# A new order of instructions for lightning attention followed by a gated MLP: step 2's keys and queries ahead of step 1's values

## The chip, the core and the metric

One core of a Trainium2 chip runs the program. Its engines have queues of their own and work side by side: TensorE (PE, with its weight loads shown as PEld), VectorE (DVE), ScalarE (ACT), GpSimd (POOL) and SyncE (SP), which here only issues DMAs. PSUM is TensorE's output memory, in eight banks; SBUF is the working memory. The metric is the device time of one execution in microseconds, from the first to the last instruction and a little around it.

## What is computed

The reference, cut to what matters. Inputs are q, k, v of 4 batches, 8 heads, 768 tokens and 64 columns, in float32:

```python
for b in range(nb):                                   # blocks of 64 tokens
    intra = np.einsum('bhic,bhjc->bhij', qb, kb) * Dmask[None]
    intra = np.einsum('bhij,bhjd->bhid', intra, vb)
    inter = np.einsum('bhid,bhde->bhie', qb * lam_pow[None], kv_state)
    out[:, :, sl] = intra + inter
    kv_state = lam_block[None, :, None, None] * kv_state + np.einsum('bhsd,bhse->bhde', kb_dec, vb)
...
x = np.ascontiguousarray(attn_out.transpose(0, 2, 1, 3)).reshape(B, S, H * D)
h = np.maximum(x @ w_in, 0.0)                         # 512 -> 1024
u, v = (h[..., :d_ff // 2].copy(), h[..., d_ff // 2:].copy())
v_n = (v - mu) / np.sqrt(var + 1e-06)                 # over the 512 columns
v_s = np.einsum('ts,bsd->btd', w_spatial, v_n) + b_spatial[None, :, None]
gated = u * v_s
return (gated @ w_out).astype(np.float32)
```

So attention with a decaying state comes first, then a layer whose normalized half is mixed over all 768 tokens of a batch by W_spatial.

## The kernel before

The tokens are cut into 12 steps of 256, three for each of the four batches; step n belongs to batch n // 3. Everything is written by small functions, one for each kind of work, and the string ORDER at the top of the file calls them one after the other: `KM.2.1.D` is the function k_m for step 2, part 1, on VectorE. The last letter names the engine (T TensorE, D VectorE, A ScalarE, P GpSimd, S SyncE), the last numbers of work on PSUM are banks. Each engine runs its own work strictly in the order of this string, and waits where data or a buffer isn't there yet. So ORDER alone decides what stands behind what.

The names, in the order in which a step uses them:

- LK, LQ, LV: loads of k, q and v of a step, 512 KB each, all on the SP queue (line 195). There are three buffers for each, so step 3 reuses those of step 0. WH: four loads of 512 KB of W_in; 0 and 1 are the half for v, 3 and 2 that for u. WQ: six loads of W_spatial, WP: W_out.
- KM, QM (line 330): scale half of a step's keys or queries by the decay and cast them to bf16 (kc, qc). VC: cast of v (vb); VD: the same in two halves. CW, CX, WC: casts of W_in and W_spatial.
- TK, TQ (line 365): transposes on TensorE into PSUM, and EK, EQ: copies of these to SBUF (kT, qT). From step 6 on DK and DQ do the transposes by DMA instead.
- SC (line 395): scores; MK (line 400): their mask, on VectorE; KP (line 424): the state's increments; SX, SY, SA: the states. AV (lines 458 and 467): the attention's output; EX: its copy to SBUF (xT). FN reads one element of a bank and holds its engine until AV's part is done.
- PV (line 492): x @ W_in for the half v; EV: its relu (vh); BN, RA, RD, RB: mean, variance, 1 / sqrt(var + eps), and -mean times that; VN: the normalized half (vn), on VectorE (line 531) or ScalarE (line 528), two to a step. PU (line 543) and EU: the half u (uT).
- WT and EW: transposes of W_spatial, once. GP: bias into a bank; PW (line 569): the spatial product over the batch's six vn tiles, eight for each batch; GM (line 575): times u (gT). PO and PH (lines 580 and 589), EO and EH, ST and SH: the output product, its copy and its store.
- FL (line 308): matmuls of ones whose result nobody reads.

A PV matmul reads both halves that EX writes: PV.n.0 first that of EX.n.0, PV.n.1 first that of EX.n.1. The vn of a batch are all needed by each of its PW; the matmuls of one PW read them in the order of the tokens.

Of the kernel before, what the change touches and what calls it, by code (L numbers as in the profile page):

```python
# [13 lines left out]


ORDER = """
lam.A BR.A tab.0.A LQ.0.S LK.0.S LQ.1.S LV.0.S LK.1.S LV.1.S LK.2.S LQ.2.S WH.0.S WH.1.S posk.P msk.P idn.P eps.D
one.D row.D FL.1.512.3.1.T FL.1.512.0.1.T LB.0.T FL.1.512.1.1.T FL.1.512.1.1.T FL.1.512.2.1.T FL.1.256.5.1.T
BB.1.6.T BB.0.1.T LN.0.A LL.D LX.A KM.0.1.D QM.0.0.P TQ.0.0.4.T QM.0.1.D KM.0.0.D TQ.0.1.3.T TK.0.0.2.T TK.0.1.5.T
FL.1.512.0.1.T EQ.0.0.4.D mkc.D EQ.0.1.3.D EK.0.1.5.D QM.1.1.D QM.1.0.P BE.0.1.A BE.1.6.A EK.0.0.2.A tab.1.A  # L20
SC.0.0.1.2.T MK.0.0.1.2.D VC.0.P KP.0.4.T SC.0.1.5.6.T TQ.1.0.0.T KM.1.0.P KM.1.1.P TQ.1.1.2.T TK.1.0.1.T
FL.1.512.3.1.T FL.1.512.3.1.T FL.1.256.3.1.T SX.0.A SY.0.4.A SA.0.1.D MK.0.1.5.6.D KM.2.1.D TK.1.1.3.T
FL.1.512.4.1.T EQ.1.0.0.A AV.0.0.5.6.T EQ.1.1.2.A EK.1.0.1.A FN.0.5.6.A EK.1.1.3.A VD.1.1.P VD.1.0.P KP.1.4.T
SC.1.0.0.1.T SY.1.4.D AV.0.1.5.6.T FL.1.512.2.1.T FL.1.512.2.1.T KM.2.0.P SC.1.1.3.4.T FL.1.512.2.1.T MK.1.0.0.1.D
QM.2.0.P QM.2.1.P CW.2.P EX.0.1.6.A EX.0.0.5.A TK.2.1.6.T FL.1.512.0.1.T FL.1.256.1.1.T TK.2.0.2.T TQ.2.0.5.T
FL.1.256.0.1.T TQ.2.1.1.T SA.1.1.D MK.1.1.3.4.D EQ.2.0.5.D CW.0.D SA.1.0.D EK.2.1.6.A EK.2.0.2.A AV.1.0.6.3.T
SC.2.0.4.5.T MK.2.0.4.5.D EQ.2.1.1.A LV.2.S WH.3.S WH.2.S LK.3.S FN.1.6.3.A CW.1.A SC.2.1.0.1.T AV.1.1.6.3.T CW.3.A
PV.0.0.2.T PV.0.1.4.T CX.1.P MK.2.1.0.1.D EV.0.1.4.D EX.1.0.6.A EX.1.1.3.A PV.1.0.5.T PV.1.1.0.T VC.2.A GP.0.3.0.3.A
KP.2.6.T AV.2.0.1.4.T EV.0.0.2.D BN.0.0.D EV.1.0.5.A FN.2.1.4.A EV.1.1.0.A SA.2.0.D BN.0.1.D RA.0.A GP.0.0.0.6.D
BN.1.1.D BN.1.0.D RD.0.D RB.0.D PU.1.1.2.T AV.2.1.1.4.T PU.0.1.5.T EX.2.1.4.A EX.2.0.1.A PV.2.1.0.T EU.1.1.2.A  # L30
RA.1.A EV.2.1.0.A LQ.3.S CX.0.P PU.1.0.4.T EU.1.0.4.A EU.0.1.5.A PV.2.0.1.T EV.2.0.1.A QM.3.1.D BN.2.1.D VN.0.1.D
BN.2.0.D WQ.1.S WQ.0.S WQ.2.S WC.2.D KM.3.0.P KM.3.1.P PU.0.0.2.T WC.0.A EU.0.0.2.A QM.3.0.P TK.3.2.0.T TQ.3.2.4.T
EQ.3.2.4.A PU.2.1.5.T WC.1.P WT.2.0.1.T WT.0.0.2.T WT.1.0.4.T EK.3.2.0.D RD.1.D RA.2.A EW.2.0.1.D RD.2.D VN.1.1.D
VN.1.0.D VN.0.0.D VN.2.1.D VN.2.0.D EW.0.0.2.A EW.1.0.4.A PU.2.0.0.T WQ.5.S LV.3.S WQ.3.S WQ.4.S EU.2.0.0.D VC.3.A
GP.0.2.0.0.A EU.2.1.5.A GP.0.1.0.5.A SC.3.1.1.2.T PW.0.0.0.6.T PW.0.3.0.3.T WC.5.P MK.3.1.1.2.D WC.3.D WC.4.P LK.4.S
LQ.4.S WP.S LV.4.S LQ.5.S PW.0.2.0.0.T WT.0.1.4.T WT.1.1.1.T WT.2.1.2.T PW.0.1.0.5.T QM.4.0.P QM.4.1.P WX.1.P
GM.0.3.0.3.D KM.4.0.D EW.1.1.1.D GM.0.0.0.6.D EW.0.1.4.A GP.0.2.1.3.A EW.2.1.2.A PW.0.2.1.3.T KP.3.4.T SC.3.0.1.2.T
GM.0.2.0.0.D GP.0.1.1.6.D GM.0.1.0.5.D SX.3.A GP.0.3.1.0.A SY.3.4.A WX.0.A GP.0.0.1.5.D KM.4.1.D MK.3.0.1.2.D
PW.0.1.1.6.T PW.0.0.1.5.T GM.0.1.1.6.D GM.0.0.1.5.D TQ.4.2.4.T PW.0.3.1.0.T GM.0.2.1.3.D SA.3.1.D GM.0.3.1.0.D
EQ.4.2.4.A TK.4.2.1.T EK.4.2.1.A PO.0.0.5.T EO.0.0.5.A VC.4.P QM.5.0.P LK.5.S KM.5.0.P KM.5.1.P QM.5.1.D PO.0.2.4.T  # L40
EO.0.2.4.D AV.3.0.6.2.T KP.4.3.T SC.4.0.0.1.T SY.4.3.D FN.3.6.2.A AV.3.1.6.2.T SC.4.1.4.5.T EX.3.0.6.A EX.3.1.2.A
PO.0.3.3.T SA.4.0.D MK.4.0.0.1.D TQ.5.2.6.T PV.3.1.2.T TK.5.2.0.T LV.5.S PV.3.0.1.T EO.0.3.3.A EQ.5.2.6.A LQ.6.S
LV.6.S LK.6.S LK.7.S LQ.7.S EV.3.1.2.A SA.4.1.D MK.4.1.4.5.D EK.5.2.0.D VC.5.P KM.6.1.P KM.6.0.P LV.7.S LK.9.S
LQ.8.S LK.8.S AV.4.0.4.0.T SC.5.0.2.3.T FN.4.4.0.A EV.3.0.1.A SC.5.1.5.6.T KP.5.6.T KM.7.0.P QM.6.1.P QM.7.0.P
QM.7.1.P KM.7.1.P GN.2.1.P QM.6.0.D MK.5.1.5.6.D AV.4.1.4.0.T PO.0.5.1.T PU.3.1.5.T EX.4.1.0.A EX.4.0.4.A PV.4.0.6.T
PV.4.1.0.T BN.3.0.D MK.5.0.2.3.D VC.6.A EO.0.5.1.D SA.5.0.D AV.5.0.4.2.T FN.5.4.2.A EV.4.0.6.A KP.6.3.T AV.5.1.4.2.T
PU.4.1.1.T PO.0.1.6.T EX.5.0.4.A EU.3.1.5.D EX.5.1.2.A PV.5.0.4.T BN.3.1.D EV.4.1.0.D BN.4.0.D SY.6.3.D BN.4.1.D
EU.4.1.1.D EV.5.0.4.A PV.5.1.5.T PO.0.4.2.T EO.0.1.6.A EV.5.1.5.A RA.4.A PU.4.0.0.T PU.5.0.3.T PU.3.0.4.T PU.5.1.1.T
BN.5.0.D GP.1.1.0.6.D BN.5.1.D EO.0.4.2.A RD.4.D VN.4.0.D GP.1.0.0.5.A GP.1.2.0.2.A RA.3.A RD.3.D RB.3.D RA.5.A
# [36 lines left out]

# [556 lines left out]
```

## Time and profile before

| | us |
|---|---|
| median of 3 runs | 142.25 (141.66 to 143.23) |
| profiled execution | 142.2 |
| its span, first to last instruction | 140.5 |
| TensorE busy in the span | 132.7 (94%) |
| VectorE busy | 114.8 (82%) |
| ScalarE busy | 80.1 (57%) |
| GpSimd busy | 55.1 (39%) |

The profile names a line of the file, an engine, an operation and its tiles. Busy time of TensorE contains its fillers (FL). In the chain of waits each piece is either an engine's work or a transfer; it shows what the end hung on, step by step back from the last instruction. The DMA share of a stage is the mean over 16 DMA engines.

### The profile page before, as it was taken

How to read it: one execution, taken by the hardware profiler on the slowest of the kernel's cores; microseconds unless marked ns; L12 is line 12 of the kernel's file. 1: busy time of each engine (PE TensorE's matmuls, PEld its weight loads, DVE VectorE, ACT ScalarE, POOL GpSimd, SP SyncE). 2: the span in 40 equal slices, each digit the busy share in tenths (PEclk: the TensorE clock that was granted, in tenths of full speed). 3: DMA queues.
4: the chain of work that ended last, by engine and by line, in shares of the span. 5: the costliest groups of instructions: out<-in, count | busy, mean ns of one | idle time of the engine just before them, and what ended most of it. 6: DMA issues, size and time to landing. Idle time of an engine off the chain costs nothing.

```text
span 140.5 us, 4680 instructions
## 1 busy us (share of the span) xinstructions
PE 132.7 (94%) x1967; PEld 84.6 (60%) x1983; DVE 114.8 (82%) x229; ACT 80.1 (57%) x160; POOL 55.1 (39%) x64
## 2 busy tenths in 40 slices
PE   5999979998999999999999999999999999999990
PEld 2367654787566657648666466586555645866540
DVE  2199889999999899999488799779899799986660
ACT  4167677799567577359532278697114476962011
POOL 5268655942578177700861419605800000000000
PEclk9999999999999999999999999999999999999999
DMA  3999999999999999998903699999865980000174
GB/s 88 345 347 347 384 370 356 379 369 357 368 346 329 325 306 277 301 161 200 285 4 76 166 347 354 283 241 218 325 175 79 364 306 7 5 2 0 41 295 186
DMA packets 56729, 34.12 MB, mean 243 GB/s; under 512 B 13827, under 2 KB 51971, under 8 KB 56708
## 3 DMA queue, kind: packets, MB, share of 16 engines
q1 hardware_dynamic: 56560, 33.69, 81.4%
q8 instruction: 15, 0.25, 0.7%
q10 hardware_dynamic: 148, 0.13, 0.3%
q14 instruction: 6, 0.05, 0.2%
HBM read 24.38 MB, written 6.29 MB: 218 GB/s over the span
## 4 chain that ended last, share of the span: by engine, by line
PE 82%; SPq 6%; DMA 5%; DVE 2%; POOL 1%; issue 1%; ACT 1%; ACTq 0%; POOLq 0%
PE ps L569 23%; PE ps L492 15%; PE ps L543 15%; PE ps L580 14%; SPq L195 6%; DMA q_in<-in_q_dram 5%; PE ps L467 4%; PE ps L395 3%; PE ps L458 3%; PE ps L365 2%; PE ps L424 2%; POOL qc L330 1%; DVE vn L531 1%; PE ps L555 1%; PE ps L589 1%
## 5 line engine op out<-in xcount | busy, mean ns | idle before, releaser
L569 PE MATMUL ps<-wt_sb,vn 128*128 128x384 bf16 x192 | 33.0, 326 | 0.4 <-DVE vn L531 0.4
L400 DVE TENSOR_TENSOR a_sb<-ps,m 128x1024 bf16<-128x1024 f32 x24 | 28.7, 1216 | 1.0 <-PE ps L395 0.8
L569 PEld LDWEIGHTS <-vn 128*128 128x128 bf16 x192 | 18.3, 98 | 12.2 <-DVE vn L531 0.7
L330 POOL TENSOR_TENSOR qc<-q_in,lqn 128x512 bf16<-128x512 f32 x18 | 19.5, 1099 | 14.0 <-DMA q_in<-in_q_dram 7.7
L543 PE MATMUL ps<-xT,win_sb 128*128 128x256 bf16 x192 | 23.1, 273 | 0.0
L492 PE MATMUL ps<-win_sb,xT 128*128 128x512 bf16 x92 | 22.5, 379 | 0.3 <-issue 0.2
L580 PE MATMUL ps<-wout_sb,gT 128*128 128x512 bf16 x82 | 21.3, 380 | 0.6 <-issue 0.2
L575 DVE TENSOR_TENSOR gT<-ps,uT 128x384 bf16<-128x384 f32 x32 | 16.7, 551 | 5.7 <-PE ps L569 5.6
L543 PEld LDWEIGHTS <-win_sb 128*128 128x128 bf16 x192 | 18.4, 98 | 3.9
L330 POOL TENSOR_TENSOR kc<-k_in,lv 128x512 bf16<-128x512 f32 x18 | 18.9, 1064 | 2.8 <-DMA k_in<-in_k_dram 1.4
L180 ACT ACTIVATE o_sb<-ps 128x512 f32<-128x512 f32 (+1 forms) x16 | 9.2, 580 | 17.4 <-PE ps L580 9.9
L507 DVE BATCH_NORM_STATS2 st<-vh 128x6 f32<-128x512 bf16 x24 | 16.4, 683 | 1.0 <-ACT vh L497 0.8
L180 ACT ACTIVATE ps<-bsp 128x384 f32<-128x384 f32 x23 | 11.1, 489 | 8.5 <-DVE gT L575 7.7
L180 ACT ACTIVATE xT<-ps 128x512 bf16<-128x512 f32 x23 | 12.5, 592 | 5.3 <-PE ps L467 5.3
L492 PEld LDWEIGHTS <-xT 128*128 128x128 bf16 x96 | 9.0, 98 | 9.5 <-ACT xT L180 1.3
L580 PEld LDWEIGHTS <-gT 128*128 128x128 bf16 x92 | 8.5, 98 | 9.1
L184 POOL CAST vb<-v_in 128x1024 bf16<-128x1024 f32 (+1 forms) x9 | 8.6, 964 | 12.8 <-PE ps L467 7.8
L497 ACT ACTIVATE vh<-ps 128x512 bf16<-128x512 f32 x18 | 10.5, 593 | 3.2 <-PE ps L492 3.2
L467 PE MATMUL ps<-a_sb,vb 64*64 64x128 bf16 x384 | 9.9, 217 | 0.0
L395 PE MATMUL ps<-qT,kT 64*64 64x128 bf16 x384 | 9.8, 226 | 0.0
L497 ACT ACTIVATE uT<-ps 128x512 bf16<-128x512 f32 x16 | 9.2, 589 | 0.3 <-PE ps L543 0.3
L395 PEld LDWEIGHTS <-kT 64*64 64x64 bf16 x384 | 6.9, 111 | 1.9 <-issue 1.3
(77 smaller groups left out, 168.8 us busy)
## 6 DMA issues: line engine op xcount, KB each, us to landing
q_in<-in_q_dram SPq DMA_DIRECT2D x12, 512.0 KB, 7.0
k_in<-in_k_dram SPq DMA_DIRECT2D x12, 512.0 KB, 6.4
v_in<-in_v_dram SPq DMA_DIRECT2D x12, 512.0 KB, 6.3
out_dram<-o_sb SPq DMA_DIRECT2D x23, 256.0 KB, 3.0
wst<-in_moe_w_in_dram SPq DMA_DIRECT2D x4, 512.0 KB, 8.2
wst<-in_moe_w_spatial_dram SPq DMA_DIRECT2D x4, 384.0 KB, 6.5
wst<-in_moe_w_out_dram SPq DMA_DIRECT2D x1, 1024.0 KB
wss<-in_moe_w_spatial_dram SPq DMA_DIRECT2D x2, 384.0 KB, 6.1
```

The lines of the kernel that those rows point to most:

```text
L180: nc.scalar.activation(out=o, in_=i, func=AF.Copy)
L330: vec(e).tensor_tensor(out=dst[n % NCA][:, u].rearrange("p u m o d -> p o (u m) d"), in0=src[n % NIN].rearrange("p (o u) m d -> p o u m d" ...
L395: nc.tensor.matmul(out=pa[o][row(c), w, j], lhsT=kT[n % NTR][row(o), u, j, c * Q64:(c + 1) * Q64], rhs=qv(n, o, u, c), start=(w == 0 and j ...
L400: nc.vector.tensor_tensor(out=a_sb[n % NA][:, i].rearrange("p o w j x -> p o w (j x)"), in0=ps[:, b0:b1 + 1:b1 - b0].rearrange("p o (w y) ...
L467: nc.tensor.matmul(out=po[c ^ o][row(w), c, i], lhsT=vb[n % NCA][row(c), 4 * o + u, j, :], rhs=a[row(c), i, o, w, j, :], start=(r == 0 and ...
L492: nc.tensor.matmul(out=bank(b), lhsT=x[:, slot(c, g)], rhs=win_sb[:, g, DH:DFF], start=(g == 0), stop=(g == NCH - 1))
L497: nc.scalar.activation(out=o, in_=i, func=AF.Relu)
L507: nc.vector.bn_stats(out=st6[p2][:, t], in_=vh[p2][:, t])
L543: nc.tensor.matmul(out=pu[:, f2].rearrange("p (c x) -> p c x", c=2), lhsT=win_sb[:, g, f * P:(f + 1) * P], rhs=x[:, slot(0, g):slot(1, g) ...
L569: nc.tensor.matmul(out=bank(b)[:, 0:HW], lhsT=vn[bb % 2][:, s, f * P:(f + 1) * P], rhs=wt_sb[:, s, i * HW:(i + 1) * HW], start=False, stop ...
L575: nc.vector.tensor_tensor(out=gT[bb % 2][:, f, cols], in0=bank(b)[:, 0:HW], in1=uT[bb % 2][:, f, cols], op=ALU.mult)
L580: nc.tensor.matmul(out=bank(b), lhsT=gT[bb % 2][:, f, t * P:(t + 1) * P], rhs=wout_sb[:, f, :], start=(f == 0), stop=(f == NCH - 1))
```

## The change

Only ORDER changes: the functions are the same (one empty line less at the top moves all line numbers down by one). All engines get a new order. Counted over the string:

| kind | before | after |
|---|---|---|
| VN | 18 on VectorE, 6 on ScalarE | 14 and 10 |
| EV | 6 on VectorE, 18 on ScalarE | 11 and 13 |
| EX | 1 on VectorE, 23 on ScalarE | 3 and 21 |
| EO | 8 on VectorE, 15 on ScalarE | 10 and 13 |
| EU | 8 on VectorE, 16 on ScalarE | 9 and 15 |
| EQ | 3 on VectorE, 6 on ScalarE | 5 and 4 |
| QM | 6 on VectorE, 18 on GpSimd | 3 and 21 |
| WC | 2 VectorE, 1 ScalarE, 3 GpSimd | 0, 2 and 4 |
| VD | 2 GpSimd | 1 GpSimd, 1 ScalarE |
| CX | 2 GpSimd | 1 GpSimd, 1 ScalarE |
| FL | 17 on TensorE | 10 |

Two lines of the table, the ones with the first loads:

```diff
-lam.A BR.A tab.0.A LQ.0.S LK.0.S LQ.1.S LV.0.S LK.1.S LV.1.S LK.2.S LQ.2.S WH.0.S WH.1.S posk.P msk.P idn.P eps.D
+lam.A BR.A tab.0.A msk.P idn.P posk.P LK.0.S LQ.0.S LQ.1.S LV.0.S eps.D one.D row.D FL.1.512.1.1.T FL.1.256.0.1.T
```

The SP queue from its start, before; q_in, k_in and v_in with their buffer's number are the loads of the steps, wst_0 and wst_1 take W_in:

```order
L195 DMA q_in_0_90<-in_q_dram 128x8x128
L195 DMA k_in_0_93<-in_k_dram 128x8x128
L195 DMA q_in_1_91<-in_q_dram 128x8x128
L195 DMA v_in_0_96<-in_v_dram 128x8x128
L195 DMA k_in_1_94<-in_k_dram 128x8x128
L195 DMA v_in_1_97<-in_v_dram 128x8x128
L195 DMA k_in_2_95<-in_k_dram 128x8x128
L195 DMA q_in_2_92<-in_q_dram 128x8x128
L252 DMA wst_0_141<-in_moe_w_in_dram 128x2x512 x2
L195 DMA v_in_2_98<-in_v_dram 128x8x128
L252 DMA wst_1_142<-in_moe_w_in_dram 128x4x256 x2
L195 DMA k_in_0_93<-in_k_dram 128x8x128
```

The same stretch after:

```order
L194 DMA k_in_0_93<-in_k_dram 128x8x128
L194 DMA q_in_0_90<-in_q_dram 128x8x128
L194 DMA q_in_1_91<-in_q_dram 128x8x128
L194 DMA v_in_0_96<-in_v_dram 128x8x128
L194 DMA k_in_1_94<-in_k_dram 128x8x128
L194 DMA k_in_2_95<-in_k_dram 128x8x128
L194 DMA q_in_2_92<-in_q_dram 128x8x128
L194 DMA v_in_1_97<-in_v_dram 128x8x128
L251 DMA wst_0_141<-in_moe_w_in_dram 128x2x512 x2
L251 DMA wst_1_142<-in_moe_w_in_dram 128x4x256
L194 DMA v_in_2_98<-in_v_dram 128x8x128
L194 DMA q_in_0_90<-in_q_dram 128x8x128
```

v_in_1 (LV.1) goes from the sixth to the eighth place, k_in_2 and q_in_2 move up one each, and the first of the two loads into wst_1 moves ahead of v_in_2.

ScalarE ahead of the first PV, before; qT, kT are EQ and EK, seen2 is FN, xT is EX, win_sb is CW:

```order
L180 ACTIVATE seen2_73<-ps_61 1x1
L180 ACTIVATE kT_1_106<-ps_61 128x512
L180 ACTIVATE xT_0_115<-ps_61 128x4x128 x2
L180 ACTIVATE kT_0_105<-ps_61 128x512 x2
L180 ACTIVATE qT_0_107<-ps_61 128x512
L180 ACTIVATE seen2_73<-ps_61 1x1
L180 ACTIVATE win_sb_84<-wst_0_141 128x512 x2
L180 ACTIVATE xT_1_116<-ps_61 128x4x128 x2
```

The same place after:

```order
L179 ACTIVATE seen2_73<-ps_61 1x1
L179 ACTIVATE vb_1_104<-v_in_1_97 128x512
L179 ACTIVATE xT_0_115<-ps_61 128x4x128 x2
L179 ACTIVATE kT_0_105<-ps_61 128x512 x2
L179 ACTIVATE seen2_73<-ps_61 1x1
L179 ACTIVATE win_sb_84<-wst_0_141 128x512 x2
L179 ACTIVATE xT_1_116<-ps_61 128x4x128 x2
```

Half of the cast of v_in_1 (VD.1.0) came to ScalarE, ahead of both EX of step 0, both EK of step 2 and two CW; the copy qT_0 (EQ.2.1) left for VectorE.

ScalarE ahead of batch 2's first PW, before; vh is EV, uT is EU, rstd is RA, vn is VN, o_sb is EO, ps<-bsp is GP, ysb is SY:

```order
L497 ACTIVATE vh_0_118<-ps_61 128x512
L180 ACTIVATE ysb_0_139<-ps_61 128x256
L180 ACTIVATE o_sb_8_134<-ps_61 128x512
L497 ACTIVATE vh_0_118<-ps_61 128x512
L528 ACTIVATE vn_0_120<-vh_0_118,nmr_0_75,rstd_0_81 128x512 x2
L512 ACTIVATE rstd_0_81<-mv_0_79,eps_t_74 128x2
L497 ACTIVATE uT_0_122<-ps_61 128x2x256
L528 ACTIVATE vn_0_120<-vh_0_118,nmr_0_75,rstd_0_81 128x512
L180 ACTIVATE ps_61<-bsp_88 128x384
```

The same place after:

```order
L496 ACTIVATE vh_0_118<-ps_61 128x512
L496 ACTIVATE uT_0_122<-ps_61 128x2x256
L511 ACTIVATE rstd_0_81<-mv_0_79,eps_t_74 128x2
L496 ACTIVATE vh_0_118<-ps_61 128x512
L179 ACTIVATE ps_61<-bsp_88 128x384
L527 ACTIVATE vn_0_120<-vh_0_118,nmr_0_75,rstd_0_81 128x512 x2
L511 ACTIVATE rstd_0_81<-mv_0_79,eps_t_74 128x2
L179 ACTIVATE o_sb_8_134<-ps_61 128x512
L527 ACTIVATE vn_0_120<-vh_0_118,nmr_0_75,rstd_0_81 128x512
L179 ACTIVATE ps_61<-bsp_88 128x384
```

Between EV.8.0 (the first row) and ScalarE's last v_n of the batch, now VN.8.0 and before VN.8.1, stand one EU, two RA, one EV, one GP, one EO and two other v_n; before, between EV.8.0 and VN.8.1, one SY, one EO, one EV, two other v_n, one RA and one EU. On VectorE RB.8, which VN on ScalarE needs, stands behind VN.6.0, RD.8 and VN.6.1. On TensorE, between the batch's last PV (PV.8.1) and its first PW, stand PU.8.0, PO.1.2, PU.7.0, PU.6.0 and PU.8.1; before there were five PU.

131 lines of the change are left out of this document (65 added, 66 removed).

## The prediction

> **What bounds the kernel now.** I read the page's first two parts, then busy time by stage, then the chain of work that ended last, then the order of time up to the first dense matmuls, and last the place where TensorE meets VectorE and ScalarE before a spatial product. Busy time by stage, with the columns stretch, its length, PE, PEld, DVE, ACT and POOL busy, clock, DMA share, GB/s:
>
> ```profile
> 14.00:18.78 4.78, 4.02 (x128) 2.66 (x126) 4.24 (x7) 2.92 (x6) 3.67 (x4) 1.00 1.09 375
> 18.78:20.77 1.99, 1.83 (x84) 1.56 (x86) 1.45 (x3) 1.56 (x4) 0.61 (x1) 1.00 1.11 384
> 20.77:36.00 15.23, 14.81 (x190) 10.28 (x191) 14.29 (x33) 12.70 (x24) 7.67 (x8) 1.00 1.08 364
> 36.00:67.00 31.00, 30.69 (x516) 20.36 (x519) 29.52 (x58) 20.81 (x41) 16.33 (x16) 1.00 1.07 287
> 67.00:95.50 28.50, 28.34 (x454) 17.95 (x456) 23.02 (x50) 16.29 (x36) 13.44 (x14) 1.00 0.83 222
> 95.50:124.00 28.50, 28.18 (x423) 17.73 (x425) 25.60 (x53) 15.57 (x34) 5.03 (x5) 1.00 0.61 177
> 124.00:136.90 12.90, 12.82 (x75) 7.15 (x73) 8.65 (x16) 2.60 (x7) 0.00 (x0) 1.00 0.23 90
> ```
>
> From 20.77 on TensorE is idle for 0.42 + 0.31 + 0.16 + 0.32 + 0.08 = 1.3 us in 116. Its real work is the same before and after, so three things alone can move the end: when the dense part starts, how much idle time is left in it, and the 3.6 us behind the last matmul. The chain, with start, length and what:
>
> ```profile
> 9.39 7.16 DMA q_in<-in_q_dram
> ...
> 16.68 2.06 POOL qc L330 x2
> ...
> 18.78 0.40 PE ps L365 x4
> ...
> 20.77 3.40 PE ps L492 x15
> 24.17 0.31 PE ps L424 x12
> ```
>
> The dense part hangs on step 2's queries, the eighth load of the SP queue: they land at 16.5 (9.39 + 7.16), GpSimd scales them, TensorE transposes them, and the first PV starts at 20.77. How the loads come, and what the engines do around the start (order of time):
>
> ```profile
> 4.99 1.04 POOL L330 TENSOR_TENSOR qc<-q_in,lqn 128x512 bf16<-128x512 f32 x1 [2.02 <-DMA q_in<-in_q_dram]
> 7.97 1.27 POOL L330 TENSOR_TENSOR qc<-q_in,lqn 128x512 bf16<-128x512 f32 x1 [1.95 <-DMA q_in<-in_q_dram]
> ...
> 13.01 1.16 POOL L184 CAST vb<-v_in 128x512 bf16<-128x512 f32 x2
> 13.98 0.74 DVE L330 TENSOR_TENSOR kc<-k_in,lv 128x512 bf16<-128x512 f32 x1 [0.31 <-DMA k_in<-in_k_dram]
> 16.68 2.04 POOL L330 TENSOR_TENSOR qc<-q_in,lqn 128x512 bf16<-128x512 f32 x2 [1.05 <-DMA q_in<-in_q_dram]
> 17.15 1.21 ACT L180 ACTIVATE kT<-ps 128x512 bf16<-128x512 bf16 x2 [0.36 <-PE ps L365]
> 19.10 0.61 POOL L184 CAST win_sb<-wst 128x512 bf16<-128x512 f32 x1 [0.38 <-DMA wst<-in_moe_w_in_dram]
> 19.46 0.81 PE L395 MATMUL ps<-qT,kT 64*64 64x128 bf16 x32
> 19.76 1.13 ACT L180 ACTIVATE win_sb<-wst 128x512 bf16<-128x512 f32 x2
> 20.80 1.05 ACT L180 ACTIVATE xT<-ps 128x512 bf16<-128x512 f32 x2
> ```
>
> The first load is there by 4.99, the third by 7.97, the seventh by 13.98: (13.98 - 4.99) / 6 = 1.5 us each. The eighth should follow at 15.4 and comes 1.1 later. In that stretch one packet of the instruction queue sits on the DMA engines (its row of the stretch 13.8 to 15 us):
>
> ```profile
> q8 instruction: 1, 0.02, 4.9%
> ```
>
> 4.9% of 16 engines x 1.2 us is 0.94 us of one engine. A load is whole when its slowest engine is done, so this one packet accounts for most of the 1.1 us, as I read it; the trace does not name the packet's engine.
>
> **The change part by part.** *Loads.* k2 and q2 move up one place each and v1 goes from sixth to eighth; the two copies of W_in's second half keep places nine and ten. By the spacing above k2 comes at 12.5 and q2 at 14.0. GpSimd's four scalings of step 2 take 4 x 1.04 us and end at 16.7 instead of 18.7, so the wait that carries the chain now is gone. Late next is v1. If its place decides, it lands at 16.5; if the delay belonged to q2, at 15.4. I take 16.5, since place eight is again followed by W_in, and TensorE's instructions up to there are as many within a few rows, so the instruction packet comes near the same time.
>
> What is queued behind v1: half of its cast (VD.1.0) is now on ScalarE, in front of EX.0.1, EX.0.0, EK.2.1, EK.2.0, CW.0 and CW.1, all of which TensorE needs. From the rows: 16.5 + 0.6 (half of 1.16) = 17.1; two EX 1.05, 18.2; two EK 1.21, 19.4; two CW 1.13, 20.5; two EX of step 1 1.05, 21.6. On TensorE, SC.2 needs the EK and takes 0.81, to 20.2; PV.0.0 has its first matmul then, its second waits for CW.1 until 20.5. CW.2 and CW.3 on VectorE hang on the ninth and tenth load as before (19.1) and are ready by 20.3. PV.1.1, now second of the four PV, meets EX.1 at 21.1 to 21.6 where the first PV ends at 21.2. The four end at 24.0 to 24.1, against 24.17: 0.1 us won. With v1 at 15.4 the whole ScalarE queue is 1.1 earlier and 1.2 us are won.
>
> *Up to the first spatial product.* WH.3 now comes ahead of LV.2 and LQ.3, and WH.2 behind them; by the spacing (WH.1 at 19.1, then 20.5, 22.0, 23.4, 24.9) the GpSimd cast for PU.1.1 is ready at 21.6 (1.04 us, as in the rows of lines 184 and 330), before TensorE gets to it at 24. CX.0 for PU.1.0 moves to ScalarE, behind four EV, one GP, one EU; its 1.05 us could make TensorE wait 0.3 us at 27.4. Against that, the wait for v_n ahead of the first product goes:
>
> ```profile
> 35.13 3.10 PE L569 MATMUL ps<-wt_sb,vn 128*128 128x384 bf16 x18 [0.36 <-DVE vn L531]
> ...
> 41.33 0.45 PE L424 MATMUL ps<-vb,kc 64*64 64x64 bf16 x32
> ```
>
> The 0.36 us is covered, because KP.3 (0.45 us as shown), behind the first products until now, stands in front of them. I put this stretch at 0.2 us won. Start and this stretch: 0.3 us with v1 at 16.5, 1.4 us with v1 at 15.4.
>
> *Fillers.* Seven of the FL groups go (17 to 10), all before 20 us, in gaps where TensorE waits for loads: nothing on the path, except for the clock (below). *Tail.* The last four are again PO and EO of batch 3, the last copy on ScalarE, the last store on SP: no difference.
>
> *Four v_n to ScalarE.* The rows by form, with count, busy us and mean ns, and the join before batch 2's spatial product:
>
> ```profile
> L531 DVE TENSOR_SCALAR vn<-vh,mv,rstd 128x512 bf16<-128x512 bf16 x18 | 7.1, 434 | 0.0
> ...
> L528 ACT ACTIVATE vn<-vh,nmr,rstd 128x512 bf16<-128x512 bf16 x6 | 4.7, 814 | 0.0
> ```
> ```profile
> 89.27 1.89 PE L492 MATMUL ps<-win_sb,xT 128*128 128x512 bf16 x8
> 90.99 4.53 PE L543 MATMUL ps<-xT,win_sb 128*128 128x256 bf16 x40
> 95.36 1.95 PE L569 MATMUL ps<-wt_sb,vn 128*128 128x384 bf16 x11
> ```
> ```profile
> 92.02 0.61 ACT L497 ACTIVATE vh<-ps 128x512 bf16<-128x512 f32 x1
> 92.49 1.53 ACT L528 ACTIVATE vn<-vh,nmr,rstd 128x512 bf16<-128x512 bf16 x2
> 93.90 0.30 ACT L512 ACTIVATE rstd<-mv,eps_t 128x2 f32<-128x2 f32 x1
> 94.09 0.60 ACT L497 ACTIVATE uT<-ps 128x512 bf16<-128x512 f32 x1
> 94.71 0.81 ACT L528 ACTIVATE vn<-vh,nmr,rstd 128x512 bf16<-128x512 bf16 x1
> ```
>
> VectorE gives up 4 x 0.434 = 1.7 us and ScalarE takes 4 x 0.814 = 3.3. That alone is no gain: from 36 us on ScalarE is idle for a third of each stage or more. What counts is the last v_n at each join. Before, PV.8.1 ends at 91.2, ScalarE's last v_n at 95.5, and the product that starts at 95.4 needs its fifth and sixth only after four matmuls of 0.16 us (1.95 / 12), at 96.0: half a microsecond to spare. After, ScalarE has from EV.8.0 to its last v_n, VN.8.0: two EV, one EU, one GP, one EO, two RA and three VN. At 0.5 us for the first five (they overlap as above, 92.02 to 92.49), 0.3 for RA and 0.75 for VN that is 2.5 + 0.6 + 2.3 = 5.4 us from 0.7 us ahead of PV.8.1's end, so VN.8.0 is done 4.7 us behind it. TensorE wants it 4.36 + 0.65 = 5.0 us behind it. The margin is 0.3 us where it was 0.5. If nothing overlaps (0.6, 0.3 and 0.81 us: 3.0 + 0.6 + 2.4 = 6.0) the wait is 0.3 us. At the joins of batches 1 and 3 the same count comes out even. I take 0.1 us for the three together, with ends 0 and 0.9.
>
> [...]
>
> *Sum.* The profiled execution took 142.2 us (span 140.5), by the median of 142.25. 142.2 - 0.3 + 0.1 = **142.0 us**: the new order wins little, since what it takes off the queries it puts on ScalarE's queue behind v1.
>
> **The rivals.**
> *A: v1 is on time.* If the eighth load lands at 15.4, ScalarE's queue shifts by 1.1 and the time is 142.2 - 1.4 + 0.1 = 140.9; without a wait at the joins 140.8. For it: the evenly spaced first seven loads. Against it: the same neighbour behind place eight.
>
> *B: VectorE becomes the bound.* Counting the table with the rows by form, VectorE loses four v_n, three q scalings, two W_spatial casts, and gets five EV, one EU, two EX, two EO, two EQ and more: about 2.5 us more in all, and from 67 to 124 about 6 us more, as its share of 36 to 67 falls. There it was busy 23.02 + 25.60 = 48.6 of 57 us; it would be 54.8. Its idle time shrinks from 8.4 to 2.2 us. Against it: between 36 and 67 it was busy 29.52 of 31.00 and TensorE still idled 0.31. It decides once less than three quarters of the idle time can be given up: with half of it, 2 us of VectorE's work come late and the time is 144.2.
>
> *C: the clock.* The filler rows show TensorE at about half rate early on:
>
> ```profile
> 9.23 0.63 PE L308 MATMUL ps<-ones 128*128 128x512 bf16 x1
> ...
> 14.12 0.38 PE L308 MATMUL ps<-ones 128*128 128x512 bf16 x1
> ```
>
> The same matmul takes 0.63 us at 9.2 and 0.38 at 14.1, though the page's clock row reads 9 throughout. If fewer fillers postpone that step to behind 24, SC.2 (0.81) and the first PV (3.40) take 0.63 / 0.38 = 1.66 times as long: 0.66 x 4.2 = 2.8 us, 145.0; with half of it 143.6. It decides from about 22 us on. Against it: from 10 to 13.6 TensorE's queue is as full as before, with SC.0, KP.0 and the transposes of step 1. [...]
>
> **How the numbers follow.** About 1%, 1.4 us, is what a measurement of this kernel can tell from no change: below 140.8, above 143.7. Forecast (142.0, own range 141.0 to 143.2) 0.52; A 0.25; B 0.16; C 0.07. A lies on the bound and is faster by over 1% in two cases of three, a sixth; the forecast's lower edge (VectorE's new order wins some of the 1.3 us idle time) adds as much as half of that: faster 0.25. B and C in four cases of five: slower 0.19. Within 1%: 0.56. The range runs from A with a little idle time won, 140.5, to half of C and near B, 143.8.
>
> **What would show it.** ScalarE's half cast of v1 begins at 16.5 (forecast) or 15.4 (A), behind idle time that ends with that load; the first PV starts near 20.2 and the four end by 24.1; the first spatial product starts at 35.1 without a wait for v_n; the one of batch 2 doesn't wait for ScalarE's v_n by more than 0.3 us. Busy VectorE from 67 to 124 near 55 us with TensorE idle under 1 us speaks against B. A filler matmul of 0.6 us behind 14 us would be C. It is wrong if TensorE idles over 2.5 us behind 21 us, or if a wait that I did not walk through (a transpose by DMA before steps 6 to 11, a bank in PSUM) ends late.

## The result, and the profile after

The changed kernel takes 141.28 us (median of 20 runs, 140.60 to 143.39); the kernel before, run beside it, 142.5 (20 runs, 141.66 to 143.23 and one of 157.45). The ratio of the faster executions of both is 0.9944, 95% interval 0.9919 to 0.9970, that of the two medians 0.9914: faster, by less than one percent. Run again later, the pair gave 141.43 and 142.63, ratio 0.9928 (0.9888 to 0.9968). The forecast was 142.0 (140.5 to 143.8). The profiled execution of the changed kernel took 141.83 us, 0.5 above the median, with a span of 140.1.

Busy time by stage in the changed kernel, in the stretches that were shown of before (same columns):

```profile
14.00:18.78 4.78, 3.76 (x160) 3.15 (x157) 4.75 (x9) 3.33 (x9) 3.06 (x4) 1.00 1.08 387
18.78:20.77 1.99, 1.94 (x49) 1.16 (x47) 1.99 (x4) 1.82 (x4) 0.47 (x1) 1.00 1.15 349
20.77:36.00 15.23, 15.18 (x227) 10.89 (x227) 14.38 (x32) 13.19 (x24) 9.08 (x10) 1.00 1.09 370
36.00:67.00 31.00, 30.12 (x480) 20.06 (x484) 26.91 (x56) 19.80 (x37) 17.18 (x19) 1.00 0.90 268
67.00:95.50 28.50, 28.19 (x453) 17.73 (x454) 26.78 (x55) 15.63 (x34) 14.17 (x15) 1.00 0.95 248
95.50:124.00 28.50, 28.18 (x421) 17.64 (x426) 26.18 (x55) 14.10 (x28) 4.53 (x4) 1.00 0.60 178
```

TensorE's idle time from 20.77 to 36 fell from 0.42 to 0.05 us, but from 36 to 67 it rose from 0.31 to 0.88. VectorE from 67 to 124 was busy 26.78 + 26.18 = 53.0 of 57 us; the prediction had counted 54.8.

ScalarE around the start of the dense part, changed kernel, in order of time:

```profile
15.56 0.61 ACT L179 ACTIVATE vb<-v_in 128x512 bf16<-128x512 f32 x1
16.26 1.09 ACT L179 ACTIVATE xT<-ps 128x512 bf16<-128x512 f32 x2
17.23 1.09 ACT L179 ACTIVATE kT<-ps 128x512 bf16<-128x512 bf16 x2
18.34 0.16 ACT L179 ACTIVATE seen<-ps 1x1 f32<-1x1 f32 x1
18.41 1.13 ACT L179 ACTIVATE win_sb<-wst 128x512 bf16<-128x512 f32 x2
19.51 1.09 ACT L179 ACTIVATE xT<-ps 128x512 bf16<-128x512 f32 x2
```

This is the queue that the prediction walked through, in the same order and with the same pieces, but it begins at 15.56 and not at 16.5: step 1's values, the eighth load, were on time. TensorE, same kernel:

```profile
19.41 3.63 PE L491 MATMUL ps<-win_sb,xT 128*128 128x512 bf16 x15
...
33.82 2.12 PE L568 MATMUL ps<-wt_sb,vn 128*128 128x384 bf16 x12
...
52.04 0.41 PE L394 MATMUL ps<-qT,kT 64*64 64x128 bf16 x14
53.13 0.24 PE L394 MATMUL ps<-qT,kT 64*64 64x128 bf16 x2 [0.67 <-issue]
...
94.52 0.81 PE L568 MATMUL ps<-wt_sb,vn 128*128 128x384 bf16 x4
95.49 1.80 PE L568 MATMUL ps<-wt_sb,vn 128*128 128x384 bf16 x10 [0.15 <-ACT vn L527]
```

The first PV starts 1.36 us earlier than before (20.77), the first spatial product 1.31 (35.13), and that one no longer waits for a v_n. Then two places give time back. In the middle of a run of score matmuls, at 52.5, TensorE does nothing for 0.67 us and waits for nothing that the profile shows ("issue"). And batch 2's product stops after four matmuls, until ScalarE's last v_n (94.62 to 95.43) is there: the next matmul would have been due at about 95.17 and starts at 95.49. At the end 0.4 us of span are won in this execution. So the questions are: is the won start the load or the new orders; are the two places the order's or this execution's; and why was the eighth load late before and not now?

### The profile page after: what moved, and what is told of

Read it like the earlier page. It is cut to its first block, busy times and chain, and to the rows that moved or that the text cites. A ratio compares the mean times of both kernels' runs of the same rounds, so it can differ in the third digit from the quotient of the medians.

```text
span 140.1 us, 4674 instructions
## 1 busy us (share of the span) xinstructions
PE 132.3 (94%) x1961; PEld 84.8 (61%) x1976; DVE 117.2 (84%) x234; ACT 79.6 (57%) x154; POOL 56.7 (40%) x65
## 4 chain that ended last, share of the span: by engine, by line
PE 57%; DMA 17%; SPq 11%; DVE 5%; POOL 3%; issue 2%; ACT 1%; POOLq 0%
PE ps L568 17%; PE ps L579 12%; DMA v_in<-in_v_dram 11%; PE ps L491 10%; PE ps L542 8%; SPq L194 8%; DMA wst<-in_moe_w_in_dram 5%; PE ps L394 3%; PE ps L466 3%; PE ps L457 2%; DVE st L506 2%; POOL vb L183 1%; DMA out_dram<-o_sb 1%; SPq L251 1%; SPq L272 1%
## 5 line engine op out<-in xcount | busy, mean ns | idle before, releaser
L329 POOL TENSOR_TENSOR qc<-q_in,lqn 128x512 bf16<-128x512 f32 x21 | 21.8, 1052 | 11.9 <-DMA q_in<-in_q_dram 7.9
L542 PE MATMUL ps<-xT,win_sb 128*128 128x256 bf16 x192 | 23.8, 273 | 0.0
L579 PE MATMUL ps<-wout_sb,gT 128*128 128x512 bf16 x84 | 21.8, 380 | 0.5 <-issue 0.2
L179 ACT ACTIVATE ps<-bsp 128x384 f32<-128x384 f32 x24 | 11.6, 490 | 10.0 <-DVE gT L574 4.8
L179 ACT ACTIVATE o_sb<-ps 128x512 f32<-128x512 f32 (+1 forms) x15 | 8.5, 565 | 14.0 <-PE ps L579 7.9
L179 ACT ACTIVATE xT<-ps 128x512 bf16<-128x512 f32 x21 | 11.6, 594 | 7.5 <-PE ps L466 7.2
L496 ACT ACTIVATE vh<-ps 128x512 bf16<-128x512 f32 x13 | 7.6, 596 | 8.0 <-PE ps L491 7.8
L394 PE MATMUL ps<-qT,kT 64*64 64x128 bf16 x384 | 10.6, 230 | 1.3 <-issue 0.7
L183 POOL CAST vb<-v_in 128x1024 bf16<-128x1024 f32 (+1 forms) x8 | 8.1, 1007 | 7.4 <-PE ps L466 5.7
L496 ACT ACTIVATE uT<-ps 128x512 bf16<-128x512 f32 x15 | 8.5, 590 | 2.2 <-PE ps L542 2.2
```

What stands on the lines that cost most here:

```text
L179: nc.scalar.activation(out=o, in_=i, func=AF.Copy)
L329: vec(e).tensor_tensor(out=dst[n % NCA][:, u].rearrange("p u m o d -> p o (u m) d"), in0=src[n % NIN].rearrange("p (o u) m d -> p o u m d" ...
L394: nc.tensor.matmul(out=pa[o][row(c), w, j], lhsT=kT[n % NTR][row(o), u, j, c * Q64:(c + 1) * Q64], rhs=qv(n, o, u, c), start=(w == 0 and j ...
L496: nc.scalar.activation(out=o, in_=i, func=AF.Relu)
L542: nc.tensor.matmul(out=pu[:, f2].rearrange("p (c x) -> p c x", c=2), lhsT=win_sb[:, g, f * P:(f + 1) * P], rhs=x[:, slot(0, g):slot(1, g) ...
L579: nc.tensor.matmul(out=bank(b), lhsT=gT[bb % 2][:, f, t * P:(t + 1) * P], rhs=wout_sb[:, f, :], start=(f == 0), stop=(f == NCH - 1))
```

## The experiments

All edits are to ORDER. The columns "first PV", "first PW" and "batch 2's first PW" give the starts of TensorE's rows in each run's trace; "us to landing" of the eighth load is from the list of DMA issues.

| run | eighth load: us to landing | first PV | first PW | batch 2's first PW | span | median of runs |
|---|---|---|---|---|---|---|
| before (shown) | 7.2 | 20.77 | 35.13 | 95.36 | 140.5 | 142.5 |
| before, second profile | 7.7 | 21.23 | 35.52 | 95.88 | 141.0 | one run, 142.72 |
| before, third profile | 7.4 | 20.96 | 35.25 | 95.86 | 141.0 | one run, 142.70 |
| before without early fillers | 6.1 | 19.42 | 33.57 | 93.58 | 138.7 | 141.20 |
| changed (shown) | 6.1 | 19.41 | 33.82 | 94.52 | 140.1 | 141.28 |
| changed, again | 6.1 | 20.84 | 35.87 | 95.74 | 141.1 | 141.43 |
| changed, PU moved | 6.1 | 19.12 | 33.52 | 94.06 | 139.5 | 141.46 |
| changed, VN.8.0 on VectorE | 6.1 | 19.37 | 33.77 | 93.64 | 138.9 | 141.59 |
| changed, both of these | 6.1 | 19.41 | 33.81 | 94.54 | 140.2 | 141.72 |
| changed, four v_n back | 6.1 | 19.32 | 34.27 | 94.25 | 139.6 | 141.93 |
| changed, v1 sixth | 6.1 | 20.71 | 35.74 | 96.88 | 142.2 | 144.08 |
| changed, 24 tiny fillers | 6.1 | 20.03 | 36.08 | 95.82 | 141.1 | 143.49 |
| changed, two more fillers | 6.0 | 19.41 | 33.81 | 94.64 | 140.2 | 141.08 |
| changed, these and VN.8.0 | 6.1 | 19.30 | 33.90 | 94.14 | 139.4 | 141.23 |

**The changed kernel again**, unchanged, as yardstick.

> The changed kernel once more, as the yardstick for its three variants on the same chip: ratio to the kernel before 0.9944 give or take 0.0025, first PV near 19.4, v1 landed at 15.35, an idle stretch of TensorE of 0.7 to 0.9 us near 52.5 in the middle of a run of 64x128 matmuls (SC of step 5) with no semaphore behind it, and 0.3 us in front of batch 2's first spatial product. If the 52.5 us gap is an accident of one profile rather than of the order, it is not there this time.

The profiled execution took 142.83 us, 1.4 above the median, and the gap at 52.5 is all but gone in it: the 16 score matmuls of SC.5.0 run in one piece of 0.55 us with a stop of 0.1 us inside (0.42 us without one), and TensorE goes from the first PW to batch 2's in 95.74 - 35.87 = 59.87 us, against 60.70 in the first profile. The stop at batch 2's product is 0.10 us here and was 0.32. This execution lost its time earlier. TensorE in it, in order of time:

```profile
14.80 0.64 PE L394 MATMUL ps<-qT,kT 64*64 64x128 bf16 x16 [0.49 <-DVE a_sb L399]
...
16.91 0.61 PE L307 MATMUL ps<-ones 128*128 128x512 bf16 x1
...
20.84 0.82 PE L491 MATMUL ps<-win_sb,xT 128*128 128x512 bf16 x3
```

and the same group of matmuls in the first profile of the same program:

```profile
14.80 0.42 PE L394 MATMUL ps<-qT,kT 64*64 64x128 bf16 x16 [0.49 <-DVE a_sb L399]
```

Up to there the two executions agree to 0.01 us. Then one runs at the faster rate (0.42 us for the group) and the other goes on at the slower one (0.64, a filler 0.61), up to about 18 us, and starts its first PV 1.43 us later; a wait of 0.46 us inside the PV for a cast of W_in follows at 22.1. That is rival C's mechanism and nearly its place, as an accident of one execution of a program, not as an effect of the change.

**A PU inside the run of small matmuls.**

```diff
-SC.5.0.2.3.T EX.4.0.4.A EX.4.1.5.A PU.3.1.6.T PV.4.0.4.T ... MK.5.0.2.3.D MK.5.1.0.1.D
+PU.3.1.6.T SC.5.0.2.3.T EX.4.0.4.A EX.4.1.5.A PV.4.0.4.T ... MK.5.1.0.1.D MK.5.0.2.3.D
```

> Changed kernel with one PU of step 3 (eight matmuls of 128x256, 1.05 us) put inside the run of about 80 small matmuls of steps 4 and 5 (in front of SC.5.0 rather than behind it; the two MK of step 5 change places on VectorE). [...] Rival 2 (a hidden wait of SC.5.0 for its bank or for the transposed keys): the gap stays in front of SC.5.0 or grows.

```profile
51.81 1.05 PE L541 MATMUL ps<-xT,win_sb 128*128 128x256 bf16 x8
52.79 0.42 PE L393 MATMUL ps<-qT,kT 64*64 64x128 bf16 x16
53.14 1.90 PE L490 MATMUL ps<-win_sb,xT 128*128 128x512 bf16 x8
55.45 1.02 PE L578 MATMUL ps<-wout_sb,gT 128*128 128x512 bf16 x4 [0.41 <-DVE a_sb L398]
```

The gap is gone, but the scores come a PU later, so does their mask on VectorE, and TensorE waits 0.41 us for it at 55.4. From the first PW to batch 2's it takes 60.54 us. The time is 141.46, ratio to before 0.9915 (0.9887 to 0.9942): no gain that can be told from the changed kernel. Since the gap is also nearly missing where nothing was moved, this run alone doesn't tell whether the PU covers it.

**VN.8.0 on VectorE.**

```diff
-VN.6.1.D RB.8.D VN.8.0.A VN.8.1.D
+VN.6.1.D RB.8.D VN.8.0.D VN.8.1.D
```

> Changed kernel with VN.8.0, the last v_n of batch 2 on ScalarE, back on VectorE, where it follows the reciprocal at 94.1 directly. Theory (the join of batch 2 waits for ScalarE's v_n of 0.81 us): the product of batch 2 runs its first six matmuls without a wait, starts at the same 94.5 and is through 0.2 to 0.3 us earlier; the time falls by 0.1 to 0.3 us. Rival (VectorE then ends late itself): the wait is as long and names VectorE, time unchanged within 0.1 us.

```profile
51.93 0.42 PE L393 MATMUL ps<-qT,kT 64*64 64x128 bf16 x16
52.29 1.05 PE L541 MATMUL ps<-xT,win_sb 128*128 128x256 bf16 x8
...
93.64 3.09 PE L567 MATMUL ps<-wt_sb,vn 128*128 128x384 bf16 x18
```

Batch 2's product runs without a stop, as expected, and so it does in the two other programs below with this edit. The starts of its matmuls, 0.16 us apart otherwise, show the stop ahead of the fifth matmul in most of the seven profiles with the v_n on ScalarE, but it is long in few: 0.32, 0.26, 0.18, 0.10, 0.05, 0.03 and 0 us. So the v_n on ScalarE is what TensorE waits for there, for 0.13 us in the mean. Up to 90 us this program is the changed kernel, and neither of the two stops is in this execution: its lead over the shown execution of before is 1.36 us at the first PW and 1.72 at batch 2's, and its span is 138.9. The lead of the start is kept to the end. The median is 141.59 (9 runs, ratio 0.993, 0.989 to 0.997): an edit worth 0.1 us in the mean can't be seen in it.

**Both edits.**

> Both edits together (the PU inside the small matmuls, VN.8.0 on VectorE). If the two stretches are what the changed kernel gave back of its earlier start, the gains add: 0.5 to 1.1 us below the changed kernel, about 140.4 us, ratio to the kernel before 0.986 to 0.991. If something behind 100 us takes up the slack, the end comes no earlier although batch 2's product does.

SC.5.0 in the profile, behind the moved PU:

```profile
53.14 0.68 PE L393 MATMUL ps<-qT,kT 64*64 64x128 bf16 x16
```

141.72, ratio 0.9944 (0.9913 to 0.9975): no gain over either edit. The stop at batch 2's product is gone, but a stop of 0.2 us is back in SC.5.0, behind its sixth matmul, so the moved PU doesn't cover it. The theory that the changed kernel gives its start back at these two places, the same in every execution, fell here: how much is lost at each differs from one execution to the next.

**The move of the loads undone.**

```diff
-LK.1.S ... LK.2.S LQ.2.S LV.1.S
+LK.1.S ... LV.1.S LK.2.S LQ.2.S
```

> Changed kernel with the move of the loads alone undone: step 1's values are loaded sixth again, step 2's keys and queries seventh and eighth; every engine's order as changed. Theory (the gain is that step 2's queries no longer come last): the eighth load, the queries, lands near 15.4 or 16.5, GpSimd scales step 2 one to two loads later (its last scaling ends near 17.5 to 18.7 and not at 16.45, and the other half of v1 behind it a microsecond later still), the first PV comes 1.5 to 2.5 us later than 19.41, the first spatial product near 35.3, and the time is 1.0 to 2.0 us above the changed kernel's, at or above the kernel before. Rival (the gain is in the new orders of the engines, wherever the loads stand): first PV within 0.5 us of 19.4, time within 0.4 us of the changed kernel's.

144.08 us, ratio to before 1.0129 (1.0063 to 1.0195): 2.7 above the changed kernel, more than expected. GpSimd, and TensorE behind it:

```profile
14.09 2.04 POOL L328 TENSOR_TENSOR kc<-k_in,lv 128x512 bf16<-128x512 f32 x2 [2.12 <-DMA k_in<-in_k_dram]
16.09 2.04 POOL L328 TENSOR_TENSOR qc<-q_in,lqn 128x512 bf16<-128x512 f32 x2
18.08 0.61 POOL L182 CAST vb<-v_in 128x512 bf16<-128x512 f32 x1
```
```profile
20.71 0.82 PE L490 MATMUL ps<-win_sb,xT 128*128 128x512 bf16 x3
22.00 2.75 PE L490 MATMUL ps<-win_sb,xT 128*128 128x512 bf16 x12 [0.46 <-DVE win_sb L180]
...
37.23 1.31 PE L567 MATMUL ps<-wt_sb,vn 128*128 128x384 bf16 x7 [0.50 <-DVE vn L529]
```

The queries land on time here as well (6.1 us), yet the new orders, which scale all of step 2 ahead of the other half of v1, lose 1.3 us at the first PV and more behind it. The new orders need the new loads; without them they are worse than the old ones.

**The kernel before without its first eleven fillers** (all FL ahead of 15 us).

> Kernel before without its eleven fillers ahead of 15 us. Two things tell apart. Packet theory: TensorE has 22 instructions fewer to run, so the instruction packet comes some 0.3 us later than 14.35, behind the data of step 2's queries, which land at 15.4 and not at 16.54; the wait of GpSimd for them shrinks by 1.1 us. Clock theory (C of the prediction): with less to do early the faster rate comes later, matmul groups behind 14 us still take 0.6 us, up to 17 or 18. If only the first holds, the first PV comes near 19.7 and the time falls by about 1 us (141.5); if only the second, the time rises by 0.5 to 2 us; if both, they meet near no change. Rival to both: queries at 16.5, rate as before, time unchanged within 0.3 us.

141.2 us (10 runs, 140.43 to 142.87), ratio 0.9927 (0.9882 to 0.9972): as much as the change, with the old orders and the old loads. The queries land after 6.1 us, and GpSimd no longer waits for them; GpSimd and TensorE in this run:

```profile
15.56 2.04 POOL L327 TENSOR_TENSOR qc<-q_in,lqn 128x512 bf16<-128x512 f32 x2
```
```profile
13.66 0.42 PE L464 MATMUL ps<-a_sb,vb 64*64 64x128 bf16 x16
...
19.42 0.82 PE L489 MATMUL ps<-win_sb,xT 128*128 128x512 bf16 x3
```

GpSimd's row began at 16.68 before, behind a wait of 1.05. The faster rate is there by 13.66 without these fillers (0.42 us for 16). From the first PW to batch 2's TensorE takes 60.01 us, in the three profiles of before 60.23 to 60.61, and with the new orders and the new loads 59.74 to 60.83: the new orders bring nothing of their own that shows behind the start.

**24 tiny fillers in the idle start** of the changed kernel (`FL.24.16.4.1.T` behind the eighth FL).

> Changed kernel with 24 tiny fillers (128x16) in TensorE's idle start (48 instructions more ahead of the loads' end), nothing else. Theory (the one instruction packet of 16 KB on the DMA engines delays the load whose data are under way when it comes, and it comes by the number of instructions that TensorE has run): the packet comes 0.5 to 1 us earlier than 14.56, while v1 or q2 is under way; v1, the eighth load, lands at 16.0 to 16.5 and not at 15.35, the first PV comes 0.5 to 1.1 us later than 19.41 and the time is 0.3 to 1.0 us above the changed kernel's. Rival (v1 is early because of its place or its size): it lands at 15.35 as before, time unchanged within 0.3 us.

The expected did not come: the instruction packet begins later, not earlier (15.12 in the trace, 14.56 in the changed kernel), and the load is on time. The time rises all the same, to 143.49 (4 runs, 141.84 to 144.70, too few and too scattered for a ratio); the profiled execution, 142.84, shows a wait that was not foreseen, for a cast of W_spatial whose load came late. GpSimd's row and TensorE's:

```profile
31.49 1.18 POOL L182 CAST wsp_raw<-wss 128x768 bf16<-128x768 f32 x1 [4.48 <-DMA wss<-in_moe_w_spatial_dram]
```
```profile
33.49 1.18 PE L553 MATMUL ps<-ident,wsp_raw 128*128 128x128 bf16 x18 [0.97 <-POOL wsp_raw L182]
```

So 48 instructions more ahead of it did not bring the packet forward in this execution.

**Two more profiles of the kernel before.**

> The kernel before, profiled once more. Theory now (step 2's queries come late because the instruction packet on the DMA engines begins at 14.35, just ahead of the end of their data; in the eight other programs profiled it began at 14.5 to 15.1 and the eighth load landed at 15.3 to 15.6): if the packet begins at or ahead of 14.4 again, the eighth load lands near 16.5, the first PV starts near 20.8 and the time is 142 to 143; if it falls behind 14.5, the queries land at 15.4, the first PV starts near 19.5 and the time is near 141. Rival (place or neighbours in the queue make the eighth load late in this kernel): 16.5 with the packet at any time.

> The same, a third execution of the kernel before, to see whether the late queries are a property of the program or of one execution: packet at 14.3 to 14.4 and queries at 16.5 a third time say that it is the program.

The queries are late in all three profiled executions (7.2, 7.7, 7.4 us to landing) and on time, or v1 in their place, in all eleven profiles of the other programs: that speaks for the program, not the execution. It need not hold for every execution, though: nine of the 91 timed executions of before took less than 141.6 us, as the changed kernel does, and none of these was profiled. The packet begins at 14.35, 14.99 and 14.57, so the bound of 14.4 fell. One thing that ties the packet to the load is a row of the DMA packets from 15.1 to 16.2 us. In the traces queries, keys and values come in packets of 512 bytes, the first two loads of W_in in packets of 2 KB, and the marks of a load's end, sixteen to a load, in packets of 4 bytes; so the packets under 2 KB less those under 512 B are what is left of the eighth load. Before, first, third and second profile:

```profile
DMA packets 227, 0.41 MB, mean 377 GB/s; under 512 B 12, under 2 KB 29, under 8 KB 227
```
```profile
DMA packets 228, 0.43 MB, mean 388 GB/s; under 512 B 10, under 2 KB 23, under 8 KB 228
```
```profile
DMA packets 221, 0.43 MB, mean 387 GB/s; under 512 B 13, under 2 KB 13, under 8 KB 221
```

and before without early fillers, and the changed kernel:

```profile
DMA packets 218, 0.43 MB, mean 387 GB/s; under 512 B 10, under 2 KB 10, under 8 KB 218
```
```profile
DMA packets 225, 0.43 MB, mean 393 GB/s; under 512 B 14, under 2 KB 14, under 8 KB 225
```

17 and 13 packets of the queries are left in two executions of before, none in the two others. In the trace the 17 come one after the other from 15.27 to 16.08, and the instruction packet of 16 KB ended at 15.28: I read them as standing behind it on one DMA engine. In the second profile no such packet is left, though the load is the latest of the three.

What settles it is the end of the loads. The trace records sixteen signals for each, and a load has landed with the last of them. In the three profiles of before fifteen signals of the eighth load are there by 15.45, 15.35 and 15.35 us, and the sixteenth comes at 16.54, 17.01 and 16.74 (first, second, third): one signal of the sixteen is late, in the second profile too. In all eleven others the sixteen are complete by 15.33 to 15.62, and it is the ninth load that has fifteen by 16.57 to 16.87 and its last at 17.67 to 18.22. So in every program the first packet, which begins at 14.35 to 15.12, goes with a delay of about 1 to 1.7 us in the last of a load's sixteen signals, and what differs is which load meets it first. The ninth is W_in's first, and in the changed kernel its cast on ScalarE begins at 18.41 without a wait. (In three variants all loads ran some 0.25 us later; there 5 to 12 packets are left at 15.1, the ordinary end of a load that took 6.1.)

**The four v_n back on VectorE** (VN.0.0, VN.0.1, VN.3.0, VN.3.1).

> Changed kernel with the four v_n (two of step 0, two of step 3) back on VectorE. If they are worth nothing, as the sum had it (0.1 us): first spatial product near 33.8 and batch 1's near 65 to 66 as in the changed kernel, VectorE 1.7 us busier and ScalarE 3.3 us less, time within 0.3 us of 141.3. If VectorE was the bound behind 20 us, so that the move to ScalarE carries the gain: the two products start 0.8 us later each and the time rises by 0.5 to 1.5 us. If ScalarE holds up the joins instead: they start earlier and the time falls by over 0.3 us.

```profile
33.67 0.44 PE L422 MATMUL ps<-vb,kc 64*64 64x64 bf16 x30 [0.29 <-ACT wt_sb L178]
33.92 0.41 PE L393 MATMUL ps<-qT,kT 64*64 64x128 bf16 x16
34.27 1.96 PE L567 MATMUL ps<-wt_sb,vn 128*128 128x384 bf16 x11
```

141.93 us, ratio 0.9992 (0.9950 to 1.0033): 0.5 to 0.65 above the changed kernel's two medians, with intervals that touch. From first PV to first PW it takes 34.27 - 19.32 = 14.95 us, the changed kernel 14.41; from there to batch 1's 31.25, as in the run with VN.8.0 on VectorE (31.16). The wait shown has its cause on VectorE: with the two v_n of step 0 in its queue, the variance of step 2 is ready at 32.6 and not at 32.1, ScalarE waits 2.2 us for it, and the copy of W_spatial behind it (wt_sb) frees TensorE's bank later. So the two of step 0 are worth 0.5 us at the first product in this execution, and the two of step 3 show nothing; one profile each doesn't say how much of it lasts in the median.

**More fillers**, and with VN.8.0 on VectorE.

```diff
-SC.1.0.5.6.T MK.0.0.0.1.D SC.1.1.1.2.T AV.0.0.3.4.T FN.0.3.4.A
+SC.1.0.5.6.T FL.1.512.3.1.T MK.0.0.0.1.D SC.1.1.1.2.T AV.0.0.3.4.T FL.1.256.0.1.T FN.0.3.4.A
```

> Changed kernel with two more filler matmuls (128x512 and 128x256) in the two idle places of TensorE between 14.3 and 15.7 us. Why: the same kernel took 141.83 us in one profiled execution, where 64x128 matmuls (16 of them) went from 0.64 us a group to 0.42 by 14.8 us, and 142.83 us in another, where they still took 0.64 at 14.8 and the first PV came at 20.84 and not at 19.41. Theory C' (the step of TensorE's rate comes at another time in each execution, and a less busy TensorE ahead of it puts it off to 18 us in some of them): with the idle places filled the slow rate is gone by 15.5 us, the first PV starts by 19.5, executions above 142 us become rare, the median falls by 0.2 to 0.5 us (to about 141.0). Rival 1 (what TensorE does there has no bearing on the step): the median and the spread stay, 141.3 to 141.4 and up to 142.8. Rival 2 (the fillers are in the way): the first PV and the median come 0.2 to 0.4 us later.

> Changed kernel with the two more fillers ahead of 16 us and with VN.8.0 on VectorE: 140.8 to 141.1 us, no execution above 142, ratio to the kernel before 0.988 to 0.993; batch 2's product without a wait for a v_n. If the join of batch 2 was not worth anything, 141.1 as with the fillers alone.

141.08 (ratio 0.9931, 0.9894 to 0.9969) and 141.23 (0.9937, 0.9899 to 0.9975): none is faster than the changed kernel by what can be measured. Of the changed kernel's 31 executions 7 took over 142 us, of the 24 of these two programs one. That is in favour of fillers against the late rate, and too few to show it. The gap at 52.5 is back in both profiles, 0.69 us of "issue" in the first (shown) and 0.23 in the second:

```profile
52.02 0.36 PE L394 MATMUL ps<-qT,kT 64*64 64x128 bf16 x12
53.07 0.25 PE L394 MATMUL ps<-qT,kT 64*64 64x128 bf16 x4 [0.69 <-issue]
```

It stands behind the 12th matmul of SC.5.0 in both. In both profiles of the changed kernel and in the run with v1 sixth it stands behind the 14th; in the run with both edits, where a PU of eight matmuls comes first, behind the 6th. Two matmuls more ahead of it move it by two, eight by eight: so in these six profiles it has its place at a fixed number of TensorE's instructions, whatever matmul is there, and it is no wait of SC.5.0 for its data or its bank. Nothing tried here took it away for certain.

## Why the prediction was right, and where it was wrong

*The number and the mechanism.* The time lies in the stated range, but that range was drawn to hold rival A as well, and A, at a chance of 0.25, is what happened; the mechanism that the 142.0 was built on, at 0.52, is not. That the time fell inside the range owes more to the range's width than to the sum.

*What bounds it.* Right: the gain is the start of the dense part, and most of it was kept. In the execution without the two stops the lead is 1.36 us at the first product, 1.72 at batch 2's and 1.6 in span, on a difference of medians of 142.5 - 141.28 = 1.2. The 0.2 us put down for the stretch up to the first product don't show: it takes 14.41 us from the first PV, and took 14.36. And the end is not quite "no difference": from batch 2's first product to the last instruction the four profiles of the old order take 45.1 us, the ten of the new order 45.3 to 45.7, of which the wait for a v_n is up to 0.3.

*The loads.* This step failed: "I take 16.5, since place eight is again followed by W_in, and TensorE's instructions up to there are as many within a few rows, so the instruction packet comes near the same time." The packet does come near the same time (14.56 against 14.35), but the load, issued at 9.29, has landed at 15.35. That the packet goes with the delay is borne out by the sixteen signals in all fourteen profiles; that its start alone decides which load it meets is refuted (14.57 late, 14.56 on time). In the first profile of before the packet takes 0.93 us, to 15.28, and from 15.27 on the last 17 packets of the queries come one after the other; I read both as being on one DMA engine, which the trace does not name. The span of before has 15 such packets of 16 KB beside 3,950 matmuls and weight loads of TensorE. No run here shows which instructions a packet holds, nor what sets when it is asked for. What lets it meet the eighth load in one program and the ninth in another stays open.

*Rival A* is what happened: v1 on time, the ScalarE queue 0.9 to 1.1 earlier at each piece than the forecast had it, PV at 19.41. It had 140.9; the medians say 141.3, from a base that turned out 142.5. The forecast of 142.0 was 0.7 too high: with the start worth 1.4 and not 0.3, and the base 0.3 higher, its sum gives 141.2.

*The joins.* Right in place and size. They were put at 0.1, with ends 0 and 0.9, and the wait ahead of the fifth matmul of batch 2's product is 0 to 0.32 us in the seven profiles with that v_n on ScalarE, 0.13 in the mean, and 0 in the three with it on VectorE. The wait of 0.3 us feared for PU.1.0 at 27.4 doesn't show, and the covered wait for a v_n at the first product went as predicted.

*Four v_n.* "That alone is no gain" fits what step 3 shows; the two of step 0 gain 0.5 us at the first product in the one profile that undoes them, because VectorE is not idle enough there (above).

*Rival B* is refuted: VectorE has 53.0 of 57 us, and TensorE idles 0.31 + 0.32 = 0.63 there, part of it for ScalarE. *Rival C* is not what the change did: in the profile of before without eleven of the fillers the faster rate is there at 13.66 (0.42 us for 16 matmuls). But single executions get it late, and one that did so at 18 us lost 1.4 us at the first PV, half of what C had for 24 us. No run shows what brings the step.

*The new orders.* The sum had them worth little beside the start. The runs say the same from the other side: old orders with the queries on time 141.2, new orders with v1 on time 141.3, new orders with the old loads 144.1. The old orders with the new loads were not run.

## What to carry to other kernels

When the last of a row of equal loads comes late and its neighbours don't, look at what else was on the DMA engines in that microsecond before reordering the work: here taking out fillers, which moved no load, brought the same 1.3 us as a new order of the whole program. And before explaining a stop of under a microsecond in one profile, profile the same program again: of the two stops that the first profile showed, 0.7 and 0.3 us, the next execution had 0.1 us each. Where a stop moves with the number of instructions ahead of it, as the one of SC.5.0 did from behind the 14th matmul to behind the 12th with two matmuls more ahead, the data of the matmul that it stands at are not its cause. A single part undone must be undone with what was fitted to it, or it measures the misfit (144.1 us).

## What the runs showed of the hardware

The step to TensorE's faster rate came at different times in two executions of one program. In the changed kernel a group of 16 score matmuls at 14.80 took 0.42 us in one and 0.64 in the next, which went on so up to 18 us, though TensorE had been busy for 12.76 of the 13.25 us before it in both; the granted clock is 1.00 in both.

In all fourteen profiles one packet of 16 KB of the instruction queue, 0.88 to 0.94 us long, goes with a delay in a 512 KB load: the last of its sixteen signals comes 0.9 to 1.7 us behind the fifteenth. GpSimd, which waits for the whole load, lost 1.05 us by it in the kernel before.

An idle stretch of TensorE marked "issue" within one run of equal matmuls was 0.67 us long in one execution of the changed kernel and 0.1 in the next. Here it goes with the instruction packet just ahead of it. In six executions TensorE stopped at the place in SC.5.0 named above, for 0.1 to 0.9 us between the starts of two matmuls, and went on 1.25 to 1.58 us behind the end of that packet (it ended at 51.68 in the changed kernel's first profile, and TensorE went on at 53.13). In three others it came to the same place 1.8 to 2.2 us behind the packet's end and did not stop. I read it as matmuls that waited for the packet; no run moved a packet on purpose, so it is not shown. Nor does it fit every place: in the run with both edits a stop of 0.4 us at 99.8 ended 0.6 us behind its packet.
